# A banded attention with a feed-forward layer: attention weights turned by three whole-width transposes and moved through DRAM, weights loaded by chunk

## The chip, the cores and the metric

One Trainium2 chip, one of its cores. The time is that of one launch on the device in microseconds; the median of several runs counts. A profile of one execution was taken beside them. The engines are named as in the profile: PE (TensorE: matmuls), DVE (VectorE), ACT (ScalarE), POOL (GpSimd) and SP (SyncE, which here only issues transfers).

## The reference

```python
def _attn_ref(q, k, v):                      # 8 batches, 8 heads, 576 tokens, 64 per head
    scores = scale * np.matmul(q, k.transpose(0, 1, 3, 2))
    rel = pos[:, None] - pos[None, :]
    mask = (rel >= 0) & (rel < 64)
    scores = np.where(mask, scores, -1000000000.0)
    attn = np.exp(scores - np.max(scores, axis=-1, keepdims=True))
    attn = attn / (np.sum(attn, axis=-1, keepdims=True) + 1e-09)
    return np.matmul(attn, v)

def _moe_ref(x, w_in, w_out):                # 4608 tokens, 512 -> 2048 -> 512
    h = x @ w_in
    g = np.where(h >= 1, h, np.where(h <= -1, 0.0, (h + 1) ** 2 / 4))
    return g @ w_out
```

The output of the attention, heads side by side, is the input `x` of the second function. All is float32. Each token sees itself and the 63 before it.

## The kernel before

**Tiles.** The 4608 tokens are nine tiles of 512. Each tile has four attention steps of 128 tokens (`s` = 0 to 35), and a feed-forward part over 16 chunks of 128 hidden columns (`f` = 0 to 15).

**A step of attention.** SP loads queries, keys and values (`load_q`, `load_k`, `load_v`). PE makes the scores in PSUM (`att_scores`, L409). From step 7 on the tokens are taken in groups of 32, each of which sees 96 keys. DVE adds the mask (`att_masked`, L426) and finds the maximum (L430); ACT takes the exponentials in eight calls (`att_exp`, L437); DVE inverts the sums (L444, L445); DVE or POOL multiply (`att_normalize`, L449). Then the weights, which lie with queries on the partitions, have to be turned so that keys lie there. From step 8 on `att_transpose_both` (L455) does it with twelve transposes on DVE, each of which turns blocks of 32 x 32 from 32 partitions to 32 others: for each of four groups of queries the three groups of keys. PE then multiplies them with the values (`att_values`, L484). Every matrix product of the feed-forward part runs in two parts of reduced width, a high one and a low one (`xh`, `xl`; `gh`, `gl`).

**Tiles 0 and 1.** Here the feed-forward part uses the weights directly: 12 matmuls of 128 x 512 for the first layer (`ffn_in`, L873), `relu`, square and gate on ACT and DVE (L885, L890, L897), the split of the gate into `gh` (ACT, L902) and `gl` (L907), and 12 matmuls for the second layer into four accumulators `acc` (`ffn_out`, L924). The weights come in a 64-bit form: SP loads them (`w_load`), ACT and DVE turn them into two float parts each (`w_rest` to `w_low`). For `f` below 4 the two units (first and second layer) are loaded one by one; later ones come in pairs of two `f` of one unit (`add_weights`). A key `gates` makes each gate follow the one before it.

**Sums.** During tile 1 the first layer's weights are prepared for tiles 2 to 8, where two chunks are done with seven products in place of eight. For each of eight pairs `n` SP copies three blocks as they are to DRAM in six transfers (`sum_pass`, L723), POOL or DVE form sums in a tile `half` (L734, L743), ACT and DVE split them into `o` and `half` (L265, L753), and SP stores these to DRAM (`sum_keep`, L758, L759). The `o` buffers (two) also carry the output of a tile from `acc` to the store (L955).

**Tiles 2 to 8.** SP loads the prepared weights for each pair from DRAM (`ring_load`, L796); PE makes the products (`ffn_products`, L824) in PSUM banks `ps_h`; ACT and DVE collect them into `h` (L265, L840); then gate and second layer as above. Step 8 to 35 bring the inputs for tiles 2 to 8; their values go through `x_take` and `add_build` into the operands of the seven products.

**What sets the order.** A planner (`Plan`) is run in Python before anything is issued. Each piece of work has a key, a planned cost on one engine or a choice of engines, what it follows, and the buffers that it takes and gives back. The planner goes through the engines and emits the work; each engine then runs its own instructions strictly in that order, waiting on semaphores. So every constant of the table at the head (W_LATE, S_LATE, keys) moves instructions on all engines. Transfers are issued by SP, in its order; only the first keys and the first weights are issued by ACT.

Of the kernel before, what the change touches and what calls it, by code (L numbers as in the profile page):

```python
# [41 lines left out]
W_PAIR = 0, 2.0  # L42
# [9 lines left out]
FIRST_LOAD = 0, 1, 0  # L52
# [31 lines left out]
BUFS = dict(qt=2, kt=2, vt=4, ps_a=2, sm=2, ptd=3, pt2=1, x=2, u=2, ps_h=2, a=2, gh=2, gl=2, acc=4, o=2, h=2, ra=2, rb=2, tmp=2)  # L84
# [3 lines left out]
S_LATE = 2  # L88
S_LATER = 2
# [7 lines left out]
IN_A = "w6_0", "w8_0"  # L97
IN_B = "w10_0", "w12_0"
H_SLOT = "w4_0"
# [3 lines left out]
A_EARLY = 5  # L103

# [89 lines left out]
def banded_attention_then_ffn(ctx: ExitStack, tc: tile.TileContext, q, k, v, w, masks, out, dims):  # L194
# [4 lines left out]
    NF = 2 * w.shape[0]  # L199
# [24 lines left out]
    nmsk = const.tile([P, 3, WIN], F32, name="nmsk")  # L224
    idr = const.tile([P, P], F32R, name="idr")
    mskr = const.tile([P, 3, WIN], F32R, name="mskr")
# [18 lines left out]

    ptq = const.tile([P, BUFS["ptd"], NP, SB], F32, name="ptd")
    ptd = [ptq[:, i] for i in range(BUFS["ptd"])]
# [31 lines left out]
    def w_load(g, eng=nc.sync):  # L279
        f, nf, u = g  # L280
        m = nf * DM
        ws[g] = t = wpool.tile([P, 4 * m], U16, name="raw", tag=f"w{f}_{u}")
        src = w[f // 2, :, u, f % 2:f % 2 + nf].bitcast(U16)
        eng.dma_start(out=t[:, :4 * m - 1], in_=src.rearrange("p f n -> p (f n)")[:, 1:])

    def w_sign(g):

        m = g[1] * DM  # L290
# [21 lines left out]
    def w_rest(g):  # L312

        m = g[1] * DM
# [8 lines left out]
    def w_high(g, eng):  # L323
        f, nf, u = g
        ws[g] = t = wpool.tile([P, nf, 2, DM], F32R, name="wts", tag=f"w{f}_{u}")
        for j in range(nf):
            wts[f + j, u] = t[:, j]
        us[g] = us[g].bitcast(F32).rearrange("p (u n) -> p u n", n=DM)
        copy(eng, t[:, :, 0], us[g])
# [7 lines left out]
    def add_weights(f, nf, unit):  # L337
        g = f, nf, unit
        m = nf * DM
        act, high, join, low, small = 105 + .916 * m, 92 + .844 * m, 10 + 1.22 * m, 67 + 1.05 * m, 90 + .25 * m  # L340
        key = f * W_STEP - (W_FIRST[f] if f < len(W_FIRST) else W_LEAD) + (W_PAIR[unit] if nf == 2 else .5 * unit)
        x = add(W0_KEY + W0_STEP * (f + .5 * nf * unit), dict(SP=W_LOAD * nf), lambda e: None if g == FIRST_LOAD else w_load(g), lag=DMA_LAG)
# [8 lines left out]
        for j in range(nf):  # L351
            w_ready[f + j, unit] = x
# [14 lines left out]
    def pt_of(s, h):  # L367
        return h if s >= SOON else (2 * seq[s] + h) % len(ptd)
# [5 lines left out]
    def near(s):  # L374
        return s >= PE_STEPS
# [14 lines left out]
    def load_masks():  # L390
        nc.sync.dma_start(out=nmsk[:, :, :NEAR], in_=masks)

    def round_masks():
        nc.scalar.copy(idr, idt)
        nc.scalar.mul(mskr[:, :2], msk[:, :2], 1.0 / scale)
# [26 lines left out]
    def att_masked(s, h):  # L422
        ps, sm, _, _ = blk[s, h]
        m = nmsk[:, variant(s), :NEAR] if near(s) else msk[:, variant(s)]
# [26 lines left out]
    def att_transpose_both(s, i, j, c):  # L451
        r = slice(i * QB + j * SQ, i * QB + (j + 1) * SQ)
        src = blk[s, BOTH][1][r].rearrange("p h a n -> p (h a) n")
        dst = ptq[(c + j) * SQ:(c + j + 1) * SQ, :2].rearrange("p h a n -> p (h a) n")
        nc.vector.transpose(dst[:, :, r], src[:, :, c * SQ:(c + 1) * SQ])  # L455
# [19 lines left out]
    def att_values(s, pool):  # L475

        vt, pt = [vts.pop((s, i)) for i in range(2)], [ptd[pt_of(s, h)] for h in range(2)]
        vals[s] = ps = banks_of_heads(pool)
        for p in range(NP):
            for i in range(2):  # L480
                n = slice(i * QB, (i + 1) * QB)
                for h in range(2):
                    c = (2 * p + h) * D
                    nc.tensor.matmul(  # L484
                        ps[half[h], p, n], lhsT=vt[i][:, c:c + D], rhs=pt[h][:, p, n], start=True, stop=True
# [13 lines left out]

    xfs, xops = {}, {}  # L500
# [7 lines left out]
    def x_tiles(t):  # L508
# [3 lines left out]
        a, b = (xpool.tile(shape, F32R, name="xs", tag=f"{n}{t % 2}") for n in ("xh", "xl"))  # L512
        if t % 2:
            c = wpool.tile(shape, F32R, name="xs", tag="w14_0")
            rest = [c[:, 0], c[:, 1], wpool.tile(shape[:1] + shape[2:], F32R, name="xs", tag="w3_0")]
        else:
            rest = [wpool.tile(shape[:1] + shape[2:], F32R, name="xs", tag=f"w{f}_0") for f in range(3)]
# [67 lines left out]
    def add_step(t, i):  # L585
# [77 lines left out]
        else:  # L663
# [7 lines left out]
            x += last["t"] + early_values  # L671
            pieces_ = [(i, j, c) for i in range(2) for j in range(QB // SQ) for c in range(NEAR // SQ)]
# [46 lines left out]
    def sum_pass(n):  # L719
        f0, f1 = by_chunk(n)  # L720
        for part in range(2):
            for o, w_, e in (0, f0, 0), (5, f0, 1), (6, f1, 1):
                nc.sync.dma_start(out=kept[n][:, part, :, o], in_=w_[:, part, :, e].bitcast(F32))  # L723
# [418 lines left out]
```

## Time and profile before

| | us |
|---|---|
| median of 3 runs (lowest, highest) | 906.59 (905.62, 907.96) |
| the profiled execution's own time | 907.99 |
| its span, first to last instruction | 906.2 |
| PE busy in the span | 875.5 |
| DVE busy | 656.1 |
| ACT busy | 506.8 |
| POOL busy | 264.2 |
| mean granted clock of PE | 0.987 of full |

The profile gives, for each engine, when an instruction ran, and for idle time what ended it. A busy PE is not always a fast one: the granted clock says how much of full speed it had. Matmuls are pipelined, so groups of them are better read by the time from one group's start to the next than by the mean of one. Transfers are read from their issue on the queue of SP or ACT to their landing.

### The profile page before, as it was taken

Reading aid. Unit: us, or ns where it says so; the run is one execution under the profiler, and the core shown is the slowest. Engines: PE = TensorE matmul, PEld = TensorE weight load, DVE = VectorE, ACT = ScalarE, POOL = GpSimd, SP = SyncE. Lnnn points to the kernel's source line nnn. Section 1 sums busy time; section 2 is a strip of 40 time slices with the busy share of each in tenths; the row PEclk is TensorE's granted clock in tenths of the full one; section 3 lists DMA queues with packets and bytes.
Section 4 is the critical chain, followed back from the end, with each engine's and each line's share of the span. In section 5 each row is a group of like instructions: output and inputs, shape, how many; then the busy total and the mean of one; then the engine's idle time right before and its main releaser. Section 6 shows DMA issues by size and latency. Waiting matters only on the chain.

```text
span 906.2 us, 20363 instructions
## 1 busy us (share of the span) xinstructions
PE 875.5 (97%) x7839; PEld 762.9 (84%) x7839; DVE 656.1 (72%) x1391; ACT 506.8 (56%) x1291; POOL 264.2 (29%) x268
## 2 busy tenths in 40 slices
PE   7699997999799999999999999999999999999998
PEld 5587885887688888888898889888988888899997
DVE  6999996598977868777686767676767676833331
ACT  7998863554455555655565537454655565434343
POOL 1000034455432232423142324232413242322222
PEclk9999996999899999999999999999999999999999
DMA  9991149447567666766676658666765664557531
GB/s 333 410 377 55 54 146 291 146 157 239 198 214 226 213 199 215 253 204 193 218 251 216 216 181 285 204 204 216 260 208 194 206 228 163 164 169 237 175 117 47
DMA packets 108033, 187.60 MB, mean 207 GB/s; under 512 B 8480, under 2 KB 49696, under 8 KB 107936
## 3 DMA queue, kind: packets, MB, share of 16 engines
q1 hardware_dynamic: 107648, 185.38, 60.9%
q8 instruction: 62, 1.02, 0.5%
q10 hardware_dynamic: 288, 0.92, 0.3%
q14 instruction: 35, 0.29, 0.1%
HBM read 162.15 MB, written 24.12 MB: 206 GB/s over the span
## 4 chain that ended last, share of the span: by engine, by line
PE 75%; DVE 12%; DMA 5%; ACT 3%; issue 2%; SPq 2%; POOL 0%; ACTq 0%; DVEq 0%
PE acc L924 36%; PE ps_h L824 27%; PE ps_h L873 6%; DVE ptd L455 4%; PE ps_a L484 3%; PE ps_a L409 3%; DVE a L897 2%; DMA kept<-half 2%; DMA kt<-in_k 2%; SPq L723 1%; ACT a L885 1%; DVE h L840 1%; DVE sm L449 1%; DVE half L734 1%; DVE half L743 1%
## 5 line engine op out<-in xcount | busy, mean ns | idle before, releaser
L924 PE MATMUL acc<-wts,gh 128*128 128x512 f32 x1154 | 363.2, 396 | 2.7 <-ACT o L265 2.7
L824 PEld LDWEIGHTS ps_h<-xs,wr 128*128 128x128 f32 x2352 | 294.5, 189 | 10.3 <-DVE h L840 0.7
L824 PE MATMUL ps_h<-xs,wr 128*128 128x256 f32 x2352 | 299.2, 282 | 0.3 <-DVE h L840 0.3
L907 POOL TENSOR_TENSOR gl<-a,gh 128x512 fp32r<-128x512 f32 (+1 forms) x130 | 167.6, 1290 | 427.5 <-ACT gh L902 389.7
L924 PEld LDWEIGHTS acc<-wts,gh 128*128 128x128 f32 x1154 | 207.9, 189 | 44.6 <-ACT o L265 3.4
L924 PE MATMUL acc<-wts,gl 128*128 128x512 f32 x577 | 225.9, 391 | 0.0
L840 DVE TENSOR_TENSOR h<-h,ps_h 128x256 f32<-128x256 f32 x280 | 117.5, 420 | 127.8 <-PE ps_h L824 113.0
L902 ACT CAST gh<-a 128x512 fp32r<-128x512 f32 (+1 forms) x149 | 90.0, 604 | 133.9 <-PE acc L924 112.2
L455 DVE STREAM_TRANSPOSE ptd<-sm 32x256 f32<-32x256 f32 x336 | 146.5, 436 | 6.3
L924 PEld LDWEIGHTS acc<-wts,gl 128*128 128x128 f32 x577 | 108.7, 188 | 23.9
L885 ACT ACTIVATE a<-h 128x512 f32<-128x512 f32 x112 | 69.9, 624 | 72.3 <-DVE h L840 71.4
L897 DVE SCALAR_TENSOR_TENSOR a<-a,h 128x512 f32<-128x512 f32 x112 | 85.7, 765 | 27.7 <-ACT a L890 16.2
L873 PE MATMUL ps_h<-xh,wts 128*128 128x512 f32 (+1 forms) x296 | 93.3, 385 | 10.7 <-DVE a L897 6.6
L437 ACT ACTIVATE sm<-sm,nm 128x96 f32<-128x96 f32 (+1 forms) x256 | 93.0, 365 | 12.2 <-DVE nm L430 12.1
L890 ACT ACTIVATE a<-a 128x512 f32<-128x512 f32 (+1 forms) x139 | 85.8, 617 | 4.3
L873 PEld LDWEIGHTS ps_h<-xh,wts 128*128 128x128 f32 x296 | 56.8, 200 | 22.6 <-DVE a L897 8.1
L873 PE MATMUL ps_h<-xl,wts 128*128 128x512 f32 (+1 forms) x148 | 56.3, 380 | 0.7 <-DVE xl L497 0.6
L265 ACT COPY h<-ps_h 128x256 f32<-128x256 f32 x77 | 28.7, 372 | 47.3 <-PE ps_h L824 43.6
L549 POOL TENSOR_TENSOR xs<-u,xs 128x256 fp32r<-128x256 f32 (+1 forms) x45 | 42.3, 971 | 32.0 <-ACT xs L265 32.0
L734 POOL TENSOR_TENSOR half<-wts 128x256 f32<-128x256 f32 x12 | 9.4, 790 | 140.1 <-PE ps_h L873 123.7
L437 ACT ACTIVATION_READ_ACCUMULATOR sm<-sm,nm 128x1 f32 x256 | 47.9, 187 | 0.0
L484 PEld LDWEIGHTS ps_a<-ptd,vt 128*64 128x64 f32 x992 | 32.0, 137 | 13.1 <-DVE ptd L455 3.6
(89 smaller groups left out, 728.3 us busy)
## 6 DMA issues: line engine op xcount, KB each, us to landing
wr<-kept SPq DMA_DIRECT2D x112, 512.0 KB, 4.7
wr<-kept SPq DMA_DIRECT2D x112, 384.0 KB, 3.9
vt<-in_v SPq DMA_DIRECT2D x72, 256.0 KB, 4.9
kt<-in_k SPq DMA_DIRECT2D x35, 384.0 KB, 5.4
raw<-in_w SPq DMA_DIRECT2D x12, 1023.8 KB, 10.3
qt<-in_q SPq DMA_DIRECT2D x36, 256.0 KB, 4.8
out<-o SPq DMA_DIRECT2D x33, 256.0 KB, 4.0
kept<-wts SPq DMA_DIRECT2D x48, 128.0 KB, 2.4
```

The lines of the kernel that those rows point to most:

```text
L437: nc.scalar.activation(sm[:, p, :], (ps if masked else sm)[:, p, :], AF.Exp, bias=nm[:, p:p + 1], scale=scale if masked else 1.0, accum_ou ...
L455: nc.vector.transpose(dst[:, :, r], src[:, :, c * SQ:(c + 1) * SQ])
L484: nc.tensor.matmul(ps[half[h], p, n], lhsT=vt[i][:, c:c + D], rhs=pt[h][:, p, n], start=True, stop=True)
L824: nc.tensor.matmul(ps[:, c * 2 * SB:(c + 1) * 2 * SB], lhsT=r[:, part, cp, o], rhs=xo[k][:, xp, cp], start=i < 2 and c == 0 and j == 0 and ...
L840: nc.vector.tensor_tensor(out=h[:, to:to + 256], in0=h[:, of:of + 256], in1=ps[:, at:at + 256], op=ALU.add)
L873: nc.tensor.matmul(ps, lhsT=wts[f, 0][:, part, c * P:(c + 1) * P], rhs=x[:, c, r], start=(c == 0 and j == 0), stop=(c == NP - 1 and j == 2),)
L885: nc.scalar.activation(gs[t, f, r.start][0], phs[t, f, r.start], AF.Relu, bias=0.5, scale=0.5)
L890: nc.scalar.activation(a, a, AF.Square)
L897: nc.vector.scalar_tensor_tensor(out=a, in0=a, scalar=1.0, in1=ps, op0=ALU.min, op1=ALU.max)
L902: nc.scalar.copy(g[1], g[0])
L907: engine[eng].tensor_tensor(out=g[2], in0=g[0], in1=g[1].bitcast(F32), op=ALU.subtract)
L924: nc.tensor.matmul(acc[t, i][:, n], lhsT=g[:, sub], rhs=wts[f, 1][:, part, n], start=(q == 0 and j == 0), stop=(q == NF - 1 and j == 2 and ...
```

## The change

1. From step 8 on three transposes on all 128 partitions (`att_turn`) turn the blocks where they are, into `turned_at`. This leaves each block on the partitions of its queries. Four transfers of ACT's queue (`att_put`) write them to DRAM, and two (`att_get`) read them back with keys on the partitions, into `seen`. `att_values` reads them there. The part of `seen` that no key reaches is set to zero once (`clear_unseen`, on POOL, before step 8). Within ACT's order the loads wait for the stores to have landed, and the values wait for the loads.
2. The weights lie by chunk, and from `f` = 4 on a transfer brings both units of one `f`.
3. `sum_pass` makes three transfers of 512 rows in place of six of 256, and the sums have earlier keys (S_LATE and S_LATER 1 in place of 2).
4. The ring of prepared weights is kept in one tile per part, `h` in two single slots, and the other operands of tiles 2 to 8 in other slots; masks are narrower.
5. In tiles 0 and 1 a gate no longer follows the one before it.

The diff, cut:

```diff
-FIRST_LOAD = 0, 1, 0
+FIRST_LOAD = 0, (0,)
-S_LATE = 2
-S_LATER = 2
+S_LATE = 1
+S_LATER = 1
-IN_A = "w6_0", "w8_0"
-IN_B = "w10_0", "w12_0"
-H_SLOT = "w4_0"
+X_PIECES = (4, 5, 2), (14, 15)
+R_PIECES = (6, 8), (10, 12)
+H_SLOT = "w0_0", "w1_0"
+MOVE = 1500, 900
+MOVE_LAG = 2300, 2800
...
+    passed = [dram.tile([SB // SQ, NEAR // SQ, SQ, 2 * NP * SQ], F32, name=f"passed{n}") for n in range(2)]
...
-    ptq = const.tile([P, BUFS["ptd"], NP, SB], F32, name="ptd")
-    ptd = [ptq[:, i] for i in range(BUFS["ptd"])]
+    MOVED = 2 * NP * SQ
+    ptq = const.tile([P, (4 + NEAR // SQ) * MOVED], F32, name="ptd")
+    ptd = [ptq[:, i * NP * SB:(i + 1) * NP * SB].rearrange("p (a n) -> p a n", n=SB) for i in range(BUFS["ptd"])]
+    seen = ptq[:, :4 * MOVED].rearrange("p (g m) -> p g m", m=MOVED)
+    turned_at = ptq[:, 4 * MOVED:].rearrange("p (c m) -> p c m", m=MOVED)
+
+    def clear_unseen():
+        nc.gpsimd.memset(seen[3 * SQ:, 0:3:2], 0.0)
+        nc.gpsimd.memset(seen[:SQ, 1:4:2], 0.0)
...
-    def att_transpose_both(s, i, j, c):
-        r = slice(i * QB + j * SQ, i * QB + (j + 1) * SQ)
-        src = blk[s, BOTH][1][r].rearrange("p h a n -> p (h a) n")
-        dst = ptq[(c + j) * SQ:(c + j + 1) * SQ, :2].rearrange("p h a n -> p (h a) n")
-        nc.vector.transpose(dst[:, :, r], src[:, :, c * SQ:(c + 1) * SQ])
+    def att_turn(s, c):
+
+        src = blk[s, BOTH][1].rearrange("p h a n -> p (h a) n")
+        nc.vector.transpose(turned_at[:, c].rearrange("p (m n) -> p m n", n=SQ), src[:, :, c * SQ:(c + 1) * SQ])
+
+    def att_put(s):
+        for g in range(SB // SQ):
+            nc.scalar.dma_start(out=passed[s % 2][g].rearrange("c k m -> k c m"), in_=turned_at[g * SQ:(g + 1) * SQ])
+
+    def att_get(s):
+        src = passed[s % 2].rearrange("(i j) c k m -> j (c k) i m", i=2)
+        dst = seen.rearrange("p (i j) m -> p j i m", i=2)
+        for j in range(2):
+            nc.scalar.dma_start(out=dst[j * SQ:j * SQ + NEAR, j], in_=src[j])
...
-            for n, piece in enumerate(pieces_):
-                ends = n == len(pieces_) - 1
-                x = add(
-                    due, dict(DVE=440), lambda e, piece=piece: att_transpose_both(s, *piece),
-                    ready if ends else taken or x, takes=["pt2"] * (not n), gives=[("sm", xs)] * ends,
-                )
-                ready.append(x)
-                first = taken = taken or [x]
+            for c in range(NEAR // SQ):
+                ends = c == NEAR // SQ - 1
+                x = [add(
+                    due, dict(DVE=440), lambda e, c=c: att_turn(s, c), x + last["t"] * (not c),
+                    takes=["turned"] * (not c), gives=[("sm", xs)] * ends,
+                )]
+                if not c:
+                    [xt_] = x
+            x = [add(due, dict(ACT=MOVE[0]), lambda e: att_put(s), x, gives=[("turned", xt_)], lag=MOVE_LAG[0])]
+            if s == SOON:
+                x.append(add(due, dict(Pool=900), lambda e: clear_unseen(), early_values))
+            x = add(due, dict(ACT=MOVE[1]), lambda e: att_get(s), x, takes=["pt2"], lag=MOVE_LAG[1])
+            ready, first, taken = [x], [x], [x]
...
-        for part in range(2):
-            for o, w_, e in (0, f0, 0), (5, f0, 1), (6, f1, 1):
-                nc.sync.dma_start(out=kept[n][:, part, :, o], in_=w_[:, part, :, e].bitcast(F32))
+        for o, w_, e in (0, f0, 0), (5, f0, 1), (6, f1, 1):
+            nc.sync.dma_start(
+                out=kept[n][:, :, :, o].rearrange("p a c n -> p (a c) n"),
+                in_=w_[:, :, :, e].bitcast(F32).rearrange("p a c n -> p (a c) n"),
+            )
...
-                gates = [xg]
+                gates = [xg] if t >= PLAIN else []
...
-        for unit in range(2):
-            if f < FINE:
-                add_weights(f, 1, unit)
-            elif f % 2 == 0:
-                add_weights(f, 2, unit)
+        for units in ((0,), (1,)) if f < FINE else ((0, 1),):
+            add_weights(f, units)
```

How the order moves, at three places (a row is the line, the operation, out<-in, and the shape; x6 means six in a row).

DVE near the start, while weights for `f` = 1 to 3 are prepared (`raw`, `u`, `wts`) and the first gates are made (`a<-a,ps_h`, then `gl`). Before:

```order
L333 TENSOR_TENSOR wts<-u,wts 128x512
L298 TENSOR_SCALAR raw<-raw 128x512
L310 TENSOR_SCALAR raw<-raw 128x512
L321 TENSOR_TENSOR u<-u,raw 128x512
L298 TENSOR_SCALAR raw<-raw 128x512 x2
L333 TENSOR_TENSOR wts<-u,wts 128x512
L310 TENSOR_SCALAR raw<-raw 128x512
L897 SCALAR_TENSOR_TENSOR a<-a,ps_h 128x256
```

Now:

```order
L342 TENSOR_TENSOR wts<-u,wts 128x512
L307 TENSOR_SCALAR raw<-raw 128x512
L928 SCALAR_TENSOR_TENSOR a<-a,ps_h 128x256
L319 TENSOR_SCALAR raw<-raw 128x512
L330 TENSOR_TENSOR u<-u,raw 128x512
L938 TENSOR_TENSOR gl<-a,gh 128x256
```

The gate stands ahead of five instructions that it stood behind. In the same stretch of PE the scores of step 4 stand 30 matmuls later (24 of the first layer, 6 of the second).

SP at the change from tile 0 to tile 1, from the first passes of the weights to the stores of the first sums. Before:

```order
L723 DMA kept_93<-wts 128x2x128 x6
L723 DMA kept_94<-wts 128x2x128 x6
L723 DMA kept_95<-wts 128x2x128 x6
L723 DMA kept_96<-wts 128x2x128 x6
L758 DMA kept_93<-o 128x512
L759 DMA kept_93<-half 128x512
```

Now (`kept_95` is the same first pair):

```order
L749 DMA kept_95<-wts 512x1x128 x3
L749 DMA kept_96<-wts 512x1x128 x3
L749 DMA kept_97<-wts 512x1x128 x3
L749 DMA kept_98<-wts 512x1x128 x3
L787 DMA kept_95<-o 128x512
L788 DMA kept_95<-half 128x512
```

Twelve transfers in place of 24 stand ahead of the first stores.

A step of a later tile. DVE before, from the inverse of the sums on:

```order
L444 TENSOR_SCALAR den<-den 128x8
L445 RECIPROCAL den<-den 128x8
L449 TENSOR_TENSOR sm<-sm,den 128x384 x2
L455 STREAM_TRANSPOSE ptd<-sm 32x8x32 x5
L840 TENSOR_TENSOR h<-h,ps_h 128x256
L455 STREAM_TRANSPOSE ptd<-sm 32x8x32
L840 TENSOR_TENSOR h<-h,ps_h 128x256
L455 STREAM_TRANSPOSE ptd<-sm 32x8x32 x2
L897 SCALAR_TENSOR_TENSOR a<-a,h 128x512
L455 STREAM_TRANSPOSE ptd<-sm 32x8x32 x4
```

DVE now:

```order
L453 TENSOR_SCALAR den<-den 128x8
L454 RECIPROCAL den<-den 128x8
L458 TENSOR_TENSOR sm<-sm,den 128x384 x2
L463 STREAM_TRANSPOSE ptd<-sm 128x256 x3
L871 TENSOR_TENSOR h<-h,ps_h 128x256 x2
```

ACT now, from the second half of the exponentials on (before, no transfer stands in its order here):

```order
L446 ACTIVATE sm,den<-sm,nm 128x96 x4
L933 CAST gh<-a 128x512
L274 COPY h<-ps_h 128x256
L467 DMA passed_93<-ptd 32x3x256 x4
L916 ACTIVATE a<-h 128x512
L921 ACTIVATE a<-a 128x512
L916 ACTIVATE a<-h 128x512
L921 ACTIVATE a<-a 128x512
L933 CAST gh<-a 128x512
L473 DMA ptd<-passed_93 96x2x256 x2
L933 CAST gh<-a 128x512
```

The transposes stand in one piece, and the step's data goes on through ACT's queue: the stores after a copy of `h`, the loads five instructions later (in one step of each later tile directly behind the stores). On PE, four groups of twelve matmuls of the second layer and groups of 24, 18 and 24 of the products stand between this step's scores and its values.

More of the change, by code (lines that the diff above doesn't have):

```diff
@@ L83 @@
 PATIENCE = dict(ACT=300, DVE=0, Pool=303, PE=0, SP=0)
-BUFS = dict(qt=2, kt=2, vt=4, ps_a=2, sm=2, ptd=3, pt2=1, x=2, u=2, ps_h=2, a=2, gh=2, gl=2, acc=4, o=2, h=2, ra=2, rb=2, tmp=2)
+BUFS = dict(qt=2, kt=2, vt=4, ps_a=2, sm=2, ptd=3, pt2=1, turned=1, x=2, u=2, ps_h=2, a=2, gh=2, gl=2, acc=4, o=2, h=2, ra=2, rb=2, tmp=2)
 PLAIN = 2
-S_LATE = 2
-S_LATER = 2
+S_LATE = 1
+S_LATER = 1
 S_PACE = 2
@@ L279, in w_load @@
     def w_load(g, eng=nc.sync):
[L280 to L284, printed above, removed]
+        f, units = g
+        m = len(units) * DM
+        ws[g] = t = wpool.tile([P, 4 * m], U16, name="raw", tag=f"w{f}_{units[0]}")
+        src = w[f, :, units[0]:units[-1] + 1].bitcast(U16)
+        eng.dma_start(out=t[:, :4 * m - 1], in_=src.rearrange("p u n -> p (u n)")[:, 1:])
     def w_sign(g):
-        m = g[1] * DM
+        m = len(g[1]) * DM
         t = ws[g].bitcast(BF16)
@@ L323, in w_high @@
     def w_high(g, eng):
[L324 to L327, printed above, removed]
+        f, units = g
+        ws[g] = t = wpool.tile([P, len(units), 2, DM], F32R, name="wts", tag=f"w{f}_{units[0]}")
+        for j, u in enumerate(units):
+            wts[f, u] = t[:, j]
         us[g] = us[g].bitcast(F32).rearrange("p (u n) -> p u n", n=DM)
@@ L350, in add_weights @@
         x = add(key - W_LATE[6], dict(DVE=low), lambda e: w_low(g), [x], gives=[("u", xr)])
-        for j in range(nf):
-            w_ready[f + j, unit] = x
+        for u in units:
+            w_ready[f, u] = x
     xt = {}
@@ L730, in sum_whole @@
         else:
[L731 removed]
+            half_of[n, c] = [wpool.tile([P, 8, P], F32, name="half", tag=H_SLOT[0] if n > 2 and c else TMP_SLOT)]
         t = half_of[n, c][0]
```

82 lines of the change are left out of this document (42 added, 40 removed).

## Prediction

> **What bounds the kernel now.** I read the page first: busy times, then the chain that ended last.
>
> ```profile
> span 906.2 us, 20363 instructions
> ...
> PE 875.5 (97%) x7839; PEld 762.9 (84%) x7839; DVE 656.1 (72%) x1391; ACT 506.8 (56%) x1291; POOL 264.2 (29%) x268
> ...
> PE   7699997999799999999999999999999999999998
> ...
> DVE  6999996598977868777686767676767676833331
> ...
> DMA packets 108033, 187.60 MB, mean 207 GB/s; under 512 B 8480, under 2 KB 49696, under 8 KB 107936
> ...
> PE 75%; DVE 12%; DMA 5%; ACT 3%; issue 2%; SPq 2%; POOL 0%; ACTq 0%; DVEq 0%
> ```
>
> TensorE is the bound: 97% busy, and three quarters of the chain. The tenths show where it is not: slices 1 to 2 (the start), 7 and 11. From slice 12 on it is full. So I cut the span by stages (PE busy, PEld, DVE, ACT, POOL, then granted clock, DMA share, GB/s).
>
> ```profile
> 140.00:160.00 20.00, 13.95 (x73) 11.07 (x68) 11.81 (x24) 8.04 (x28) 10.42 (x15) 0.66 1.00 313
> 220.00:240.00 20.00, 14.92 (x150) 11.60 (x149) 19.40 (x45) 10.70 (x32) 9.95 (x14) 0.97 0.79 263
> 240.00:260.00 20.00, 20.00 (x119) 16.66 (x120) 16.57 (x36) 8.68 (x28) 7.93 (x10) 0.86 0.26 90
> 441.00:535.00 94.00, 93.58 (x914) 83.49 (x913) 70.08 (x151) 50.56 (x138) 29.20 (x25) 1.00 0.66 219
> ```
>
> A later tile takes 94.00 us with 93.58 busy at clock 1.00: 0.42 us to win in each. Around 150 us there is more: 13.95 us busy at 0.66 is 13.95 x 0.66 = 9.2 us of full-speed work in 20, so 10.8 lost. By the same sum 220 to 260 loses 20 - 14.92 x 0.97 = 5.5 and 20 x 0.14 = 2.8, together 8.3. The clock part is real time: after the 3.90 us gap shown below, twelve matmuls took 5.49 us, where twelve of the same take 2.80.
>
> ```profile
> 239.74 5.49 PE ps_h L873 x12
> 161.95 2.80 PE ps_h L873 x12
> ```
>
> **The start.** Two waits of PE, from its timeline (start, duration, what, and in brackets the idle time before and its releaser):
>
> ```profile
> 38.53 0.39 PE L873 MATMUL ps_h<-xh,wts 128*128 128x256 f32 x1 [2.08 <-DVE a L897]
> 42.51 1.10 PE L409 MATMUL ps_a<-kt,qt 64*64 64x128 f32 x32 [2.30 <-DMA kt<-in_k]
> ```
>
> The first is a gate that stood late in DVE's order; the change drops the rule that gates follow each other in tiles 0 and 1, and the gate now stands earlier. The second is the scores of step 4, put where their keys had not landed; they now stand thirty matmuls later. Both can go: 4.4 us. DVE was nearly full there (slices 2 to 6 of its tenths), so I take **-3**; bounds -4.4 and, if DVE's new order makes another matmul wait as long as the first, +2. That the later weights come one `f` at a time, both units together, leaves their bytes and their arithmetic as they were and is hidden by the same full DVE: nothing by itself.
>
> **The passes of the weights to DRAM.** SP's and POOL's rows of 122 to 142 us, and what waited:
>
> ```profile
> 122.47 14.10 SPq L723 DMA_DIRECT2D kept<-wts  x24
> 131.95 1.29 POOL L753 TENSOR_TENSOR half<-half,o 128x512 fp32r<-128x512 f32 x1
> 137.21 0.40 SPq L759 DMA_DIRECT2D kept<-half  x1
> 141.64 0.42 DVE L734 TENSOR_TENSOR half<-wts 128x256 f32<-128x256 f32 x1 [1.78 <-DMA kept<-half]
> 143.32 0.58 PE L873 MATMUL ps_h<-xh,wts 128*128 128x256 f32 x1 [2.60 <-DVE xh L267]
> 150.69 1.22 PE L924 MATMUL acc<-wts,gh 128*128 128x512 f32 x2 [2.65 <-ACT o L265]
> ACT o L265 <- DMA kept<-o: 7.2, 1, 7.2
> ```
>
> The first sums were ready at 131.95 + 1.29 = 133.2 us, but SP was issuing 24 transfers until 136.6, so they left at 137.2 and landed at 141.6. DVE stood before its next write of `half` until then, the cast `xh` stood behind that, and PE behind the cast. The second wait is the same queue: ACT could not write `o` before an earlier `o` had landed. The change sends 12 transfers ahead of that store in place of 24, each with twice the rows. What one costs to issue:
>
> ```profile
> L758 SPq DMA_DIRECT2D kept<-o x16: 319/327/438, 136.7 to 244.5; - x16
> L723 SPq DMA_DIRECT2D kept<-wts x48: 382/486/2125, 122.5 to 156.9; - x48
> ```
>
> A transfer of 128 rows takes 0.327 us, one of 256 rows 0.486. Another 0.16 for each 128 rows makes 0.81 for 512, so 12 take 9.7 us and SP is free at 122.47 + 9.7 = 132.2, before the sums are ready. Bounds: 12 x 0.49 = 5.9 us (rows cost nothing), or 14.1 as now (rows are all of the cost). The store then leaves 4 us earlier and lands about when DVE comes to its write at 139.9: the 2.60 goes. The 2.65 should shrink; how far I can't read from the order, since the stores of tile 0's output share the two `o` buffers. With the low clock that follows, I take **-8** of the 10.8; bounds -10.8 and 0.
>
> **Transposes on DVE, steps 8 to 35.** Twelve on 32 partitions become three on 128.
>
> ```profile
> L455 DVE STREAM_TRANSPOSE ptd<-sm 32x256 f32<-32x256 f32 x336 | 146.5, 436 | 6.3
> L464 DVE STREAM_TRANSPOSE ptd<-sm x24: 292/303/308, 126.5 to 137.2; 32x128 f32<-32x128 f32 x24
> L840 DVE TENSOR_TENSOR h<-h,ps_h 128x256 f32<-128x256 f32 x280 | 117.5, 420 | 127.8 <-PE ps_h L824 113.0
> ```
>
> Half as many columns take 0.303 against 0.436, so width sets the price; partitions I can bound only between 0.436 (all at once) and 4 x 0.436 = 1.74 (one block after the other). An addition of 128 x 256 takes 0.420, no more than a transpose of a quarter of the partitions, so I take 0.436: per step 12 x 0.436 = 5.23 becomes 1.31, and 28 steps save DVE 110 us. That is worth only what PE waits for it:
>
> ```profile
> 227.67 1.51 PE L484 MATMUL ps_a<-ptd,vt 128*64 128x64 f32 x32 [1.04 <-DVE sm L426]
> 239.74 0.79 PE L873 MATMUL ps_h<-xh,wts 128*128 128x512 f32 x1 [3.90 <-DVE a L897]
> by line: PE acc L924 15.9%; DVE ptd L455 14.8%; issue 12.4%; PE ps_h L873 10.4%; PE ps_h L824 8.0%; DVE a L897 7.8%; DVE xs L549 4.2%; DVE h L840 3.8%; DVE u L537 3.3%; ACT sm L437 2.7%; DVE u L267 2.4%; ACT a L885 2.3%; DVE half L743 2.3%;
> 498.89 1.04 PE L484 MATMUL ps_a<-ptd,vt 128*64 128x64 f32 x28 [0.42 <-DVE ptd L455]
> ```
>
> In the chain of 222 to 275 us transposes are 14.8%, 7.8 us, of which 9 of 12 go: 5.9. DVE is 97% busy there with tile 2's operands and the sums, so what was behind the transposes comes up by about that. Of the 8.3 lost I take **-5**; bounds -8.3 and 0. In the later tiles the one wait is 0.42 a tile on a transpose; over six tiles I take **-1**, bounds -2.5 and 0.
>
> **What is added: the way through DRAM.** Per step ACT issues four stores of 98 KB and two loads of 197 KB (28 x 0.79 = 22 MB in all, 12% more than the 187.60 MB now). An issue on ACT took
>
> ```profile
> 1.18 0.46 ACTq L284 DMA_DIRECT2D raw<-in_w  x1
> kept<-half SPq DMA_DIRECT2D x16, 256.0 KB, 2.3
> vt<-in_v SPq DMA_DIRECT2D x72, 256.0 KB, 4.9
> ```
>
> so six take 2.8 us, 11 of 94 us a tile beside ACT's 50.6: it fits. Behind the waiting loads on ACT stand casts, `relu` and the copies of `h`; a gate's cast made at 514.24 is used by PE at 523.17 (the rows below), so 3 us of delay is covered, and without that cover each us would be PE's. PE itself waits for the loads at the values. The chain, by a step of a later tile:
>
> ```profile
> 504.91 1.00 PE L409 MATMUL ps_a<-kt,qt 64*32 64x96 f32 x64
> 514.51 2.23 DVE L455 STREAM_TRANSPOSE ptd<-sm 32x256 f32<-32x256 f32 x5
> 514.24 0.62 ACT L902 CAST gh<-a 128x512 fp32r<-128x512 f32 x1 [1.58 <-PE acc L924]
> 523.17 0.73 PE L924 MATMUL acc<-wts,gh 128*128 128x512 f32 x2
> 281.22 2.75 PE acc L924 x12
> 283.97 2.85 PE ps_h L824 x24
> 279.09 2.13 PE ps_h L824 x18
> ```
>
> Scores end at 505.91 and turning starts at 514.51, 8.6 later. Then 1.3 for three transposes, 4 x 0.46 = 1.8 for the stores' issue, a landing, 0.9 for the loads' issue, a landing: 12.6 us and two landings. The new order leaves PE work for this long between a step's scores and its values: in the tightest of four steps four groups of twelve, two of 24 and one of 18, 4 x 2.75 + 2 x 2.85 + 2.13 = 18.8 us; in the others by the same sum 19.9, 21.0 and 23.3. A store lands in about 2.3 (row `kept<-half`), a load in 2.3 to 4.9 (row `vt<-in_v`, queued behind ring loads), so the chain is 17.2 to 19.8: the tightest waits 0 to 1.0 us. Over six tiles and tiles 1 to 2 I take **+2**; with the ends 0 and, at 4.4 a landing, +27 (below).
>
> The Trainium skill, "DMA: Bandwidth & Descriptors", section "Anatomy of one DMA — SWDGE (gpsimd) path", puts a transfer at about 2.0 us plus bytes over 436 GB/s, fitted on GpSimd's path: an estimate of 2.2 for a store and 2.5 for a load, by which no step waits and the sum is 2 us better. The same page's section "Issuing engines are not separate DMA queues" speaks against the change: transfers of ScalarE's queue share the 16 engines with SP's, so loads may land as late as `vt` does; the 4.9 above agrees with that.
>
> Narrower masks, ring tiles by part and single `h` slots change no duration and are hidden by PE.
>
> **Sum.** -3 - 8 - 5 - 1 + 2 = -15. The profiled execution took 907.99 us (span 906.2 and 1.8 around it), giving 893.0; it lies 1.4 over the median 906.59, so the median comes to **891.6**, own range 884 to 899.
>
> **Rivals.** First, everything comes through (0.10): -4.4 - 10.8 - 8.3 - 2.5 = -26.0 gives 880.6. For it: PE's own work is unchanged. Against it: DVE and the `o` buffers stay busy in tile 1.
>
> Second, the stall moves along (0.17): SP takes as long for 12 bigger transfers, so the first gap stays (-1 in place of -8): 898.6. For it: the same 512-byte rows in the same number. Against it: 0.327 against 0.486 shows a fixed part.
>
> Third, the slower case, the landings decide (0.14): both land later than I take. The chain beats 18.8 and 19.9 by 2.8 us a tile, which eats the gain of 17, at 20.75, that is landings of 4.1 each. At 4.4 each the chain is 21.4, the four steps wait 2.6 + 1.5 + 0.4 + 0 = 4.5, six tiles 27: 906.59 - 17 + 27 = 916.6. For it: loads of 256 KB take 4.9 now. Against it: stores take 2.3.
>
> Fourth, the transposes don't do what they should and cost four times (0.06): DVE is not relieved, -5 and -1 go, and the chain grows by 3.9 to at least 21.1, waiting 3.6 a tile, 21.6 in six: 906.59 - 11 + 21.6 = 917.2.
>
> The Trainium skill, "TensorE: Matmul & The Clock Gate", Part 1, has the clock halve after an idle window of about 3.4 us, by which waits of 2.6 at the values would cost only themselves (916.6). The trace differs: 2.60 idle at 143.32 was followed by a clock of 0.66, so by the row each such wait could cost 2.7 more, 16 in six tiles: 933.
>
> **How the numbers follow.** Forecast 0.53, rivals as above. A change of 0.3%, 2.7 us, is about what a measurement of this kernel can tell from none. Faster by more: 0.53 + 0.17 + 0.10 less 0.02 for moves that stop short = 0.78; within it 0.05, from these and the mildest landings; slower 0.17. The range 880 to 909 leaves out the two slower rivals' far side (0.17) and a little below.
>
> **What would show it.** L463 at 0.44 us; SP's first sums leaving before 135 us; no wait of 2 us on PE at 38, 143 and 235 us; a later tile still at 93.6 to 94; landings of the two moves under 4 us and waits of PE on `ptd` under 1. It is wrong if PE waits for `ptd` on a DMA by 2 us or more in each step, if ACT's copies of `h` come late behind a waiting load, or if the gaps of 140 to 160 and 220 to 260 stand elsewhere.

## The result and the profile after

The changed kernel took 933.05 us (928.06 to 937.17) beside 906.88 us for the kernel before: a ratio of 1.0287, with a 95% interval of 1.0232 to 1.0341. It is slower by 26 us, where 15 us faster was forecast. Its profiled execution took 931.63 us, with a span of 929.5. The page of that execution, the lines that answer to those of before:

```profile
span 929.5 us, 20430 instructions
...
PE 881.6 (95%) x7839; PEld 768.0 (83%) x7839; DVE 557.0 (60%) x1170; ACT 501.9 (54%) x1280; POOL 262.4 (28%) x250
...
PE   7899999998988999998999899998999899999998
...
PE 59%; DMA 12%; DVE 3%; ACTq 1%; ACT 1%; issue 1%; SPq 0%
```

DVE has lost 99 us of work (656.1 to 557.0) where 110 were forecast, and in PE's line the 6 and the 7 of slices 2 and 7 are gone. But an 8 now stands in every fourth slice or so, up to four fifths of the span, and DMA has gone from 5% to 12% of the chain that ended last. The same stretches as before, and one tile's length of 94 us (PE, PEld, DVE, ACT, POOL busy, granted clock, DMA share, GB/s):

```profile
140.00:160.00 20.00, 18.65 (x177) 14.96 (x177) 10.29 (x23) 9.35 (x20) 10.09 (x14) 1.00 1.04 326
220.00:240.00 20.00, 15.52 (x142) 11.65 (x143) 11.34 (x25) 9.09 (x27) 7.39 (x9) 0.83 0.72 220
240.00:260.00 20.00, 16.23 (x242) 14.05 (x240) 13.27 (x27) 12.05 (x39) 5.99 (x7) 1.00 0.77 245
519.00:613.00 94.00, 87.36 (x863) 77.68 (x862) 49.12 (x103) 43.01 (x112) 27.82 (x24) 0.96 0.73 231
```

The hole of 140 to 160 us is filled (18.65 us at full clock in place of 13.95 at 0.66). A later tile, which lost 0.42 us of 94 before, now loses 94 - 87.36 x 0.96 = 10.1 (the stretches of 94 us before and behind it 5.5 and 9.1 by the same sum). PE's list of waits (total, times, longest) says for what:

```profile
PE ps_a L507 <- DMA ptd<-passed: 26.3, 8, 4.5
PE ps_h L904 <- DVE a L928: 6.7, 3, 4.5
```

Eight waits of the values for the loads of the moved weights, 26.3 us, and one gate of 4.5. They are not spread over the steps. Three of them, 7.4 us, come before 300 us, and one of 2.3 us at 590. The other four, 16.6 us, stand in PE's timeline once a tile, always at the same one of its four steps, the third by its scores and the one with the least work between scores and values (19.0 us; 20.2 or more in the others). It is called the third step below:

```profile
433.49 1.15 PE L507 MATMUL ps_a<-ptd,vt 128*64 128x64 f32 x32 [3.73 <-DMA ptd<-passed]
532.74 1.97 PE L507 MATMUL ps_a<-ptd,vt 128*64 128x64 f32 x32 [4.32 <-DMA ptd<-passed]
635.00 1.98 PE L507 MATMUL ps_a<-ptd,vt 128*64 128x64 f32 x32 [4.54 <-DMA ptd<-passed]
735.41 1.98 PE L507 MATMUL ps_a<-ptd,vt 128*64 128x64 f32 x32 [3.98 <-DMA ptd<-passed]
```

Behind the last three the 32 matmuls take some 1.97 us where 1.15 is usual: the clock fell too. Behind the first it fell 1.3 us later (0.50 from 434.81 to 438.22 us). The chain of one such step, in order of time (start, us, what):

```profile
518.83 1.11 DVE ptd L463 x3
...
520.93 4.47 DMA passed<-ptd
...
526.00 6.50 DMA ptd<-passed
...
532.74 1.97 PE ps_a L507 x32
```

Turning takes 1.1 us; the two landings take 4.47 and 6.50. What else was issued then, in the timeline of SyncE, and the moves themselves in that of ScalarE:

```profile
519.90 1.02 SPq L827 DMA_DIRECT2D wts<-kept  x2
525.50 0.87 SPq L827 DMA_DIRECT2D wts<-kept  x2
```

```profile
519.96 1.91 ACTq L467 DMA_DIRECT2D passed<-ptd  x4
525.50 0.91 ACTq L473 DMA_DIRECT2D ptd<-passed  x2
```

Both hops start in the same tenth of a microsecond as a pair of ring loads (L827, the transformed weights coming back from DRAM for the products). The pairs follow the products, here 5.6 us apart; the loads follow the stores by the same 5.6. So both meet a pair, and the order being fixed, they do so in each of the four tiles of the rows above. The DMA view of 518 to 533 us (KB each, median us to landing):

```profile
wts<-kept SPq DMA_DIRECT2D x2, 512.0 KB, 6.0
...
passed<-ptd ACTq DMA_DIRECT2D x4, 96.0 KB, 4.0
ptd<-passed ACTq DMA_DIRECT2D x2, 192.0 KB, 5.8
```

The tile before these four shows the same step without the coincidence: its stores left at 326.79 us, 1.1 us ahead of a pair, and its loads from 331.01 on, ahead of the pair of 333.50. The DMA view of 322 to 336 us:

```profile
passed<-ptd ACTq DMA_DIRECT2D x4, 96.0 KB, 2.0
ptd<-passed ACTq DMA_DIRECT2D x2, 192.0 KB, 2.5
```

With a cover of 18.9 us PE did not wait there.

The gate's wait of 4.48 us at 231 us is another matter. The chain of 215 to 235 us:

```profile
221.19 6.74 DMA passed<-ptd
...
227.96 0.37 ACTq L473
...
228.37 0.63 ACT o L274
...
229.02 0.69 DVE half L782
...
230.58 0.61 DVE a L928
...
231.23 3.78 PE ps_h L904 x8
```

ScalarE stood with its loads at the head of the queue until the stores had landed. The cast `o` behind them came late, DVE's `half` behind that, the gate behind that, and PE last.

**Theory L**: the way through DRAM cost all of it, by landings longer than the work that covers them (26.3 us of waits), by the clock after them, and by ScalarE standing behind a waiting load. **Theory C**, inside it: the landings are long because ring loads are on the way at the same moment. **Rival O**: the new order and the new sharing of weight buffers cost the time, and the waits only show where. **Rival F**: the landings are the moves' own, by their bytes and rows.

### The profile page after: what moved, and what is told of

Same layout as the page of the kernel before. It is cut to its first block, busy times and chain, and to the rows that moved or that the text cites. A ratio compares the mean times of both kernels' runs of the same rounds, so it can differ in the third digit from the quotient of the medians.

```text
span 929.5 us, 20430 instructions
## 1 busy us (share of the span) xinstructions
PE 881.6 (95%) x7839; PEld 768.0 (83%) x7839; DVE 557.0 (60%) x1170; ACT 501.9 (54%) x1280; POOL 262.4 (28%) x250
## 4 chain that ended last, share of the span: by engine, by line
PE 59%; DMA 12%; DVE 3%; ACTq 1%; ACT 1%; issue 1%; SPq 0%
PE acc L955 27%; PE ps_h L855 26%; DMA ptd<-passed 5%; DMA passed<-ptd 4%; PE ps_a L507 3%; DMA wts<-kept 2%; PE ps_a L418 2%; ACTq L467 1%; DVE ptd L463 1%; PE ps_h L904 1%; DVE sm L458 1%; ACT sm L446 0%; DMA vt<-in_v 0%; ACTq L473 0%; DVE half L782 0%
## 5 line engine op out<-in xcount | busy, mean ns | idle before, releaser
L938 POOL TENSOR_TENSOR gl<-a,gh 128x512 fp32r<-128x512 f32 (+1 forms) x130 | 169.8, 1307 | 454.3 <-ACT gh L933 426.9
L955 PEld LDWEIGHTS acc<-wts,gh 128*128 128x128 f32 x1154 | 207.1, 188 | 42.4 <-DVE o L276 0.9
L855 PE MATMUL ps_h<-xs,wts 128*128 128x256 f32 x1488 | 199.6, 285 | 0.0
L855 PEld LDWEIGHTS ps_h<-xs,wts 128*128 128x128 f32 x1488 | 189.0, 193 | 0.5
L855 PE MATMUL ps_h<-wts 128*128 128x256 f32 x864 | 129.9, 287 | 0.0
L855 PEld LDWEIGHTS ps_h<-wts 128*128 128x128 f32 x864 | 120.9, 193 | 8.7
L928 DVE SCALAR_TENSOR_TENSOR a<-a,h 128x512 f32<-128x512 f32 x112 | 77.3, 690 | 45.6 <-ACT a L921 44.4
L507 PEld LDWEIGHTS ps_a<-ptd,vt 128*64 128x64 f32 x992 | 35.3, 151 | 37.9 <-issue 29.5
L507 PE MATMUL ps_a<-ptd,vt 128*64 128x64 f32 x992 | 39.6, 239 | 28.3 <-DMA ptd<-passed 26.3
L274 ACT COPY h<-ps_h 128x256 f32<-128x256 f32 x67 | 24.9, 372 | 46.1 <-PE ps_h L855 33.7
```

What stands on the lines that cost most here:

```text
L274: nc.scalar.copy(dst, src)
L507: nc.tensor.matmul(ps[half[h], p, n], lhsT=vt[i][:, c:c + D], rhs=pt[h](p, i), start=True, stop=True)
L855: nc.tensor.matmul(ps[:, c * 2 * SB:(c + 1) * 2 * SB], lhsT=r[part][:, cp, o], rhs=xo[k][:, xp, cp], start=i < 2 and c == 0 and j == 0 and ...
L928: nc.vector.scalar_tensor_tensor(out=a, in0=a, scalar=1.0, in1=ps, op0=ALU.min, op1=ALU.max)
L938: engine[eng].tensor_tensor(out=g[2], in0=g[0], in1=g[1].bitcast(F32), op=ALU.subtract)
L955: nc.tensor.matmul(acc[t, i][:, n], lhsT=g[:, sub], rhs=wts[f, 1][:, part, n], start=(q == 0 and j == 0), stop=(q == NF - 1 and j == 2 and ...
```

## The experiments

Times are medians, ratios are to the kernel before on the same chip.

**The moves left out.** In place of L465 to L473 and in the values:

```
 def att_put(s): pass
 def att_get(s): pass
-moved = seen...;       pt = moved[:, 2 * i:2 * i + 2, h, p]
+moved = turned_at...;  pt = moved[:, i:i + 2, h, p]
```

> The changed kernel with its six transfers per step left out: the values of steps 8 to 35 read the three turned blocks where DVE wrote them, so their numbers are not those of the reference, but instructions and order on PE, DVE and ACT stay. Theory L (the way through DRAM is what cost the time: PE's eight waits for the loads, 26.3 us, the lower clock after them, about 13.7 us, and the gate at 231 us behind a waiting load, 4.5 us and 3.4 of clock): 933 - 48 = about 885 us, no wait of PE over 1.5 us after 160 us. Rival O (the new order, or the new sharing of the weights' buffers, cost it): 905 us or more, with waits of PE on other lines.

It took 887.58 us, 0.9778 (0.9745 to 0.981). A stretch of 94 us from its windows tells the later tiles:

```profile
425.00:519.00 94.00, 94.00 (x917) 83.60 (x916) 56.15 (x121) 49.14 (x134) 31.03 (x26) 1.00 0.67 219
```

PE is busy for all of it, at full clock. The moves thus cost 933.05 - 887.58 = 45.5 us in an order that is otherwise the same: theory L, and against O. The sum agrees in size: 26.3 us of waits for loads, 4.5 of the gate, and lost clock (mean 0.976 over 929.5 us is 22.3 us, against 0.992 over 887.1, 7.1) make 46.0; the spans of the two profiled executions differ by 42.4.

**Twelve transposes again**, the rest of the change kept:

```
-x = add(due, dict(DVE=440), att_turn ...) x3, att_put, clear_unseen, att_get
+x = add(due, dict(DVE=440), att_transpose_both ...) x12
```

> The changed kernel with the twelve transposes per step of the kernel before in place of three and the moves; the order is planned anew. Theory L: without the moves the gains of the start and of the passes remain, 906.9 - 3 - 8 = about 896 us, with the waits of PE near 228 and 240 us back. Rival O: 915 us or more, since the rest of the change is what cost the time.

897.41 us, 0.9886 (0.9857 to 0.9915), as theory L expects: what is left of the change gains 9 to 10 us. Near 228 and 240 us, where two waits of PE were to come back, one stands (3.41 us at 230.62, on POOL's `gl`). Against the run above, turning in three rather than twelve is worth another 9.8 us, if moving cost nothing.

**The passes of the weights alone**, in the kernel before:

```
-S_LATE = S_LATER = 2
+S_LATE = S_LATER = 1
-for part in range(2): 3 transfers of 128 x (2 x 128)
+3 transfers of 128 x (4 x 128)
 (and the durations and landings that are planned for them)
```

> The kernel before with nothing but the passes of the weights in three transfers of 512 rows, their planned durations and their place one step earlier. If the pass is what emptied the stretch from 140 to 160 us: 906.9 - 8 = about 899 us, PE busy there 18 us or more of 20 at a clock of 1.00. If the stall only moves along: 905 to 908 us.

902.36 us, 0.9952 (0.9934 to 0.9971): 4.4 us, between the two expectations. The stretch did fill as the first one has it:

```profile
140.00:160.00 20.00, 17.85 (x201) 14.33 (x200) 14.81 (x33) 11.49 (x34) 11.86 (x18) 1.00 0.95 307
```

```profile
236.10 1.15 PE L484 MATMUL ps_a<-ptd,vt 128*64 128x64 f32 x32 [2.78 <-DVE sm L426]
```

The first row is from its windows, the second from PE's timeline. In that stretch 17.85 us of full-speed work stand in place of 9.2, 8.6 more, but the waits on DVE around 236 us stayed. Not all of it arrives at the end: the profiled executions differ by 6.1 us of span, the medians by 4.4. Of what is missing in the profiles 1.7 us lie in the start, where a wait of 2.40 us for the keys of step 4 (2.30 before) was followed here by a clock of 0.50 from 43.84 to 47.25 us, and of 1.00 in the kernel before. The rest is not placed.

**Longer landings in the plan.** The planner puts the values after the landings that a table counts on:

```
-MOVE_LAG = 2300, 2800
+MOVE_LAG = 4500, 6500
```

> The changed kernel with nothing but the landings that its planner counts on set to what the third steps showed: 4.5 us for the stores and 6.5 us for the loads in place of 2.3 and 2.8. Theory L (the order gave the values too little cover): PE's waits for the loads fall under 1 us each, 890 to 905 us. Rival O: 920 us or more. A third case, ACT held by its waiting loads: PE's waits go to gates and copies of h behind them, 905 to 920 us.

907.46 us, 1.0003 (0.9984 to 1.0023): 25.6 us come back, 2.5 short of the range that theory L gave. The time lies in that of the third case, but its mechanism is not what the trace shows: PE's waits on copies of `h` are 1.7 us in all, and the longest on a gate, 3.3 us at 205 us, stands behind a sum's store that took 6.65 us to land. By its windows:

```profile
441.00:535.00 94.00, 93.87 (x915) 83.45 (x914) 58.60 (x118) 49.13 (x133) 29.90 (x25) 1.00 0.77 253
...
240.00:260.00 20.00, 12.36 (x145) 10.20 (x146) 11.16 (x28) 9.22 (x40) 4.38 (x5) 0.83 0.63 199
```

The later tiles are whole again; only the cover changed, no byte and no queue. Tile 2 is worse: between 240 and 260 us PE waits 3.2 us for a load of the moves and 1.9 for operands that POOL makes, and the clock falls to 0.83. So the same numbers for the tiles from 3 on alone:

```
-lag=MOVE_LAG[0]          (and [1])
+lag=MOVE_LAG[t > PLAIN][0]   with (2300, 2800), (4500, 6500)
```

> The changed kernel with the long planned landings, 4.5 and 6.5 us, for the tiles from 3 on alone. Theory L: the later tiles lose their five long waits as in the kernel with long landings everywhere, tile 2 keeps those of the changed kernel (about 12 us of waits with the gate at 231 us, and 9 of clock): 905 to 910 us, no gain over it. If what the long landings spoil around 240 to 260 us is more than that: 895 to 903 us.

902.79 us, 0.9955 (0.993 to 0.9981): the second expectation. Before tile 3 some gate and product waits remain (4.59 us at 233 us, the longest).

**Half the bytes of the ring loads**, at the same places, and **half the bytes of the moves**, to tell C from F:

```
-dma(r[part], kept[n][:, part, :, R_OPS[i]])
+dma(r[part][:, 0], kept[n][:, part, 0, R_OPS[i]])
```

> The changed kernel with ring loads of half the bytes (only the first chunk of each is brought, so the products are not those of the reference), in the same number and at the same places; the order stays. Theory C (the pair of ring loads issued at the same moment sets when the moves land): in the third steps stores land in about 3 us and loads in about 4 in place of 4.5 and 5.8, PE's waits there fall from 4.3 to about 1.5, 905 to 915 us. Rival F (the moves' landings are their own): landings and waits as in the changed kernel, 928 to 937 us.

```
-passed[..][g], turned_at[g rows], seen[.., j], src[j]
+the same, columns [:MOVED // 2] only
```

> The changed kernel with the moves cut to half of each row (512 bytes of 1 KB; half of the weights are left behind, so the values are not those of the reference), same count of transfers and rows, same order. Theory C: the moves are 0.4 of 1.4 MB on the way at the same moment, so their landings shrink by some 0.5 us each and the time by 10 us at most: 920 to 935 us. Rival F (their own bytes set the landings): stores in about 3 us, loads in about 3.5, waits of 4.3 down to 0.5, 895 to 910 us.

With half the ring loads' bytes it took 895.7 us, 0.9884 (0.9855 to 0.9912). That is better than C asked for. The third step that was shown above, in the DMA view of this run (504 to 516 us) and in PE's timeline:

```profile
wts<-kept SPq DMA_DIRECT2D x2, 256.0 KB, 3.3
...
passed<-ptd ACTq DMA_DIRECT2D x4, 96.0 KB, 3.0
ptd<-passed ACTq DMA_DIRECT2D x2, 192.0 KB, 2.6
```

```profile
514.35 1.15 PE L507 MATMUL ps_a<-ptd,vt 128*64 128x64 f32 x32
```

The moves are the same, and land in 3.0 and 2.6 us in place of 4.0 and 5.8; none of the four third steps waits any more. One wait of 4.1 us stayed, at 255 us, where the loads still took up to 6.9 us to land. But with half the moves' bytes it took 906.19 us (899.88 to 913.87), 0.9992 (0.9962 to 1.0022), inside F's range of 895 to 910, where C had 920 at least. The moves' own bytes count for more than their share of 0.4 in 1.4 MB: in the third steps the slowest store landed in 4.0 to 4.6 us in place of 4.5 to 5.2, the slowest load in 3.9 to 4.5 in place of 5.7 to 6.6. The waits there shrank to 1 to 2 us, and the clock stayed up (the 32 matmuls behind them took 1.15 in all). So F alone can't stand, since the moves were whole when the ring loads were halved and 895.7 us was reached, and C is too small as stated: it is what is on the way together, both sides of it, and a wait that is halved saved the clock as well.

**One hop.** From one place of SBUF straight to the other:

```
-4 stores to passed, 2 loads from it
+for g in 0..3: for c in 0..2:
+    dma(seen[((g % 2) + c) * 32 : +32, g], turned_at[g * 32 : +32, c])
```

> The changed kernel with the weights moved straight from one place of SBUF to the other, by twelve transfers of 32 rows of 1 KB on ScalarE's queue, without DRAM and without a load that waits for a store. Theory L (two landings after each other are the cost): the third step's chain from the turn to the landing is 12 issues, about 4.5 us, and one landing of 4 to 6, some 9.5 us in place of the 12.6 of 520 to 532.6 us; the wait of 4.3 shrinks to about 1 and the time to 895 to 910 us. Rival: twelve issues hold ACT longer and the many small transfers land late: 920 us or more.

969.23 us, 1.0683 (1.0662 to 1.0705): the rival, which had 920 or more. The view of that line (duration ns min, median, max) and who waited for it:

```profile
L472 ACTq DMA_DIRECT2D ptd<-ptd x336: 514/601/1658, 147.6 to 844.7; - x168
...
  ACT a L915: 66.8, 8
...
  PE ps_a L506: 39.9, 20
```

One issue takes 0.60 us and not some 0.4, so ScalarE's queue is held 7.6 us or more in a step, where in the third step shown above the second hop of the changed kernel left 5.5 to 6.4 us after the first store; `relu` (L915) and the gates' casts stand behind it, and PE waits 20 times. The second landing was not the whole of the cost: what sits on ScalarE's queue counts.

**The moves on SyncE's queue**, all six or the loads alone, and all six with the longer plan from tile 3 on:

```
-nc.scalar.dma_start(...)  dict(ACT=MOVE[0])   (and [1])
+nc.sync.dma_start(...)    dict(SP=MOVE[0])
```

> The changed kernel with all six transfers of a step issued by SyncE instead of ScalarE, and planned there. Theory C (the ring loads issued beside the moves set their landings): on one queue a ring load issued behind a move comes after it, the stores land in about 2 us and the loads in about 3, PE's long waits in the third steps fall under 1.5 us, ACT never stands behind a load that waits: 890 to 905 us. Rival Q: SyncE stands at the turn and at the stores' landing, some 4 us a step, and the ring loads and vt behind it come late: PE waits on wts or vt, 915 us or more.

> The changed kernel with the two loads alone on SyncE's queue, the stores left on ScalarE's. If what counts is that ACT stands behind the waiting loads: the gate's wait of 4.5 us at 231 us and what follows it go, the third steps keep their waits of about 4: 920 to 925 us. If the loads gain from going ahead of the next ring pair: loads land in about 3 us, stores as before, waits of about 1.5: 900 to 912 us.

> All six transfers on SyncE's queue and the long planned landings, 4.5 and 6.5 us, from tile 3 on. If both cures add up: the later tiles take 94 us with no wait over 0.5, and the time is that of the better of the two alone or a little under, 888 to 900 us. If the longer plan holds SyncE's queue further apart from the work: 905 us or more.

All six took 895.59 us, 0.9872 (0.9839 to 0.9904); the loads alone 902.73, 0.9946 (0.9927 to 0.9966); all six with the longer plan 894.25, 0.9865 (0.9834 to 0.9896). A third step on SyncE, in the first of them:

```profile
503.86 1.80 SPq L467 DMA_DIRECT2D passed<-ptd  x4
505.75 0.93 SPq L827 DMA_DIRECT2D wts<-kept  x2
506.78 0.90 SPq L473 DMA_DIRECT2D ptd<-passed  x2
```

And the landings of all its stores, from the view of their line:

```profile
DMA to landing us min/median/max: 1.8/1.9/4.3
```

On one queue the ring pair goes out behind the stores; these land in 1.9 us (median of the line, 2.8 in the changed kernel), and the loads leave 2.9 us after the first store, not 5.5. The loads still follow a ring pair and land in 4.4 (median; 3.9 before), not in the 3 that were expected. PE's waits in the third steps are 0.6 us at most, the longest that the profile puts down to a load of the moves is 1.8. Rival Q hardly came: no wait on ring loads or `vt`, one of 2.9 us near 228 us; the moves' loads had left behind a ring pair and took 5.6 us to land, at 227.51, though the profile names a store of the sums that landed 0.2 us later. With the loads alone on SyncE the gate near 231 us waited 1.6 us in place of 4.5, but the gain was more than that mechanism's: the third steps waited 0.5 to 1.4 us only, the second of the expectations. Their stores were as late as before; their loads left 0.9 to 1.8 us ahead of a ring pair, not beside it, and landed in 2.4 to 2.8 us. With both, no wait of PE behind 300 us is over 1.0 us (0.5 was expected); that the two cures add up the times don't show, 894.25 beside 895.59. The Trainium skill, "DMA: Bandwidth & Descriptors", section "Issuing engines are not separate DMA queues", says that transfers interleave on the same 16 engines whichever engine issued them, so that a second queue saves only the issue. Between queues the runs agree (4.0 us beside a pair), and where it leaves out the order, they add to it: stores that went out ahead of the pair landed in 1.9. For that no common queue is needed: in the changed kernel, in a step whose stores left on ScalarE's queue at 448.69 us and met no pair before 452.60, all four landed in 1.8 to 1.9.

## Why the prediction was wrong

- **Start, -3.** The two waits went (2.08 to 0.95 us, and 2.30 to none), but the clock was lower in the first 40 us (0.83 and 0.91, after 0.91 and 1.00). PE's busy time by clock in the first 60 us went from 45.7 to 47.0: 1.3 us, inside the bounds.
- **Passes, -8.** The mechanism held. Twelve transfers took 10.66 us, 0.82 each by the line's median where 0.81 was worked out, and the first sums left at 133.35 us, before 135. Alone, the stretch itself gave 8.6 us, so the size held there too; the medians show 4.4, and part of the difference is the clock at the start.
- **DVE's relief, -5 and -1.** Too small. The turn of 128 partitions took 0.42 us, so twelve did become three at the price of one each. The two runs without moves differ by 9.8 us, where 6 were forecast.

The views of the two lines (duration ns min, median, max), and SyncE's timeline:

```profile
L463 DVE STREAM_TRANSPOSE ptd<-sm x84: 395/422/448, 142.7 to 795.6; 128x256 f32<-128x256 f32 x84
L749 SPq DMA_DIRECT2D kept<-wts x24: 512/816/1430, 122.6 to 153.5; - x24
```

```profile
122.60 10.66 SPq L749 DMA_DIRECT2D kept<-wts  x12
133.35 0.81 SPq L787 DMA_DIRECT2D kept<-o  x1
```

- **Together without the moves, -17.** Measured -19. This half of the sum was right, helped by two errors that cancel: with twelve transposes the rest gained 9.2 to 9.5 us of the 11 forecast, and turning in three gained 9.8, not 6.
- **The way through DRAM, +2.** Measured +45.5, and this step fails. It took a store's landing from the row of 256 KB stores (2.3 us) and a load's from `vt` (up to 4.9), as if a landing were a property of the transfer. In the third steps they were 4.5 and 6.5 (the rows of 520.93 and 526.00), since each was issued with a ring pair. The cover was sized rightly (18.8 us; 509.4 to 528.4, scores to values, is 19), and so was the chain without its landings (12.6 us; 12.1 in the step shown). The two landings were not: 11.0 us in place of 4.6 to 7.2. The +2 also held nothing for the clock behind a wait, some 15 us, nor for the gate, 4.5.
- **The third rival was the right one.** Its point was landings of 4.1 us, and its dearest figure, each wait lowering the clock, was 933; 933.05 was measured. That the two meet to the tenth is luck: it had two landings of 4.4 us and waits spread over the steps of six tiles, while the trace has 4.5 and 6.5 us in one step of four tiles, and a further 12 us of waits, with the gate, before 300 us. Its chance of 0.14 came from the same row of 2.3 us. That row stands for stores up to 246 us, among few ring loads. The profile of before held the warning, in SyncE's timeline of a later tile:

```profile
505.01 1.09 SPq L796 DMA_DIRECT2D wr<-kept  x2
511.74 11.33 SPq L796 DMA_DIRECT2D wr<-kept  x6
```

  Three ring pairs in 11.33 us, some 5 us apart, just where a chain of two hops was to be put; they were not set beside the new transfers.
- **ScalarE behind a waiting load** was named as a danger and covered by 3 us of slack in a later tile. It struck near 228 us, where the cast `o` of a sum stood in the queue.

## What to carry to other kernels

Take the landing of an added transfer from transfers that are issued at the same moment as the others it will meet, and look for a rhythm: a chain of two hops whose distance equals the period of another stream meets it twice, as here in four tiles in a row. A load that waits for a store should not stand on the queue of an engine that computes. If it may wait anywhere, a queue of transfers, ahead of the bulk loads, is the place: here that turned 933 us into 894 to 896, better than both kernels, though not told apart from the changed kernel with twelve transposes (897).

## What the hardware showed that was not expected

How long a wait must be to lower TensorE's clock is not one number. Behind a wait of 1.80 us in the one-hop run 28 matmuls took 1.54 us, where 1.03 is usual. A wait of 2.32 us before 589.77 us of the changed kernel left the clock alone. And the fall can come late: behind 3.10 us in the last run 32 matmuls took the usual 1.15, and then the clock was 0.50 for 3.41 us. The rows of PE's timelines, and of windows (PE's busy time comes second, the granted clock third from the end), for these three in turn:

```profile
307.80 1.54 PE L506 MATMUL ps_a<-ptd,vt 128*64 128x64 f32 x28 [1.80 <-DMA ptd<-ptd]
308.10:311.51 3.41, 3.41 (x36) 3.29 (x33) 1.79 (x4) 1.21 (x3) 1.65 (x2) 0.50 0.37 110
```

```profile
588.42:591.83 3.41, 2.06 (x40) 2.02 (x41) 0.87 (x2) 2.77 (x16) 1.30 (x1) 1.00 0.46 160
```

```profile
228.68 1.15 PE L507 MATMUL ps_a<-ptd,vt 128*64 128x64 f32 x32 [3.10 <-DMA kept<-half]
229.80:233.21 3.41, 3.41 (x9) 2.74 (x9) 2.66 (x7) 3.34 (x17) 0.00 (x0) 0.50 0.71 223
```

In every trace the granted clock is 1.00 or 0.50, and its changes lie a multiple of 3.41 us apart. So the time can be cut into windows of 3.41 us that end where the clock may change. The window that ended at 308.10 us held all of the 1.80 us, 53% of it; the one that ended at 229.80 held 2.29 us, 67%. The 2.32 us were parted between two windows: 0.97 us before 588.42 and 1.35, 40%, behind it. Over the 13 traces, from 40 to 860 us, every window at full clock that was idle for over 56% was followed by 0.50, and none that was idle for under 53%; in between both occur. PE's ends are modelled, so these shares are estimates.

The Trainium skill, "TensorE: Matmul & The Clock Gate", Part 1, has a window of 3413 ns that runs freely, and the halved clock after an idle window of some 3.4 us. The length of the window and the half agree with the traces; that it must be idle from end to end does not, since 1.80 us were enough at 308.10. The prediction read the rule as a length alone.

An issue from one place of SBUF to another, 32 rows of 1 KB, took ScalarE 0.60 us, against 0.45 for the stores to DRAM (median of L467) with three times the bytes.
